# A thresholded attention kernel: who makes the threshold of a score tile, ScalarE or VectorE

## The chip, the core and the metric

The kernel runs on one core of one Trainium2 chip. The metric is the device time of one execution in microseconds (us). Engine names are those of the profile: PE is TensorE (PEld its weight loads), DVE is VectorE, ACT is ScalarE, POOL is GpSimd, SP is SyncE, which issues most of the DMAs. The granted clock of TensorE is 1.00 (2.4 GHz) in every stretch of the profile of the kernel before.

## The reference

There are 8 batches of 8 heads, each of 576 positions by 64. For every head the scores are thresholded a little below their row maximum, and what is left goes through a softmax; the heads of a batch, side by side, are the 512 columns of `x`, which a gated mix then turns into the output:

```
scores = q @ k.T / sqrt(64)
thresh = max(scores, axis=-1) - tau
scores = where(scores >= thresh, scores, -1e9)
attn   = exp(scores - max(scores)); attn = attn / (sum(attn) + 1e-9)
x      = attn @ v                        # the heads side by side
gate   = sigmoid(causal convolution of x with 5 taps per column)
out    = (gate * (x @ w_val)) @ w_out
```

## The kernel before, in words

Heads are taken in pairs: a **job** is one pair of one batch (32 jobs, 4 per batch). Each job has 9 score **tiles** of 128 rows by 576 columns, 288 in all: four of 128 queries for each head, and one in which both heads' last 64 queries share the rows.

What a tile goes through (`class Tile`):

- **scores** (`multiply`, L538 to L558, matmuls on L556): PE writes the tile into one of the PSUM rooms `r_s`, of which there are three for the first tiles and two from then on.
- **row maximum** (`largest`, L560 to L564, instruction on L562): DVE writes minus the maximum into the first column of a small tile `nm` (128x2).
- **exponential** (`weigh`, L566 to L572): ACT computes `e = exp(s - max)` (L568). With `TH = "ACT"` ACT issues a second instruction right behind it (L570): the threshold, `nm[:, 1] = -nm[:, 0] + less`, one element for each of 128 rows, where `less` is minus tau.
- **keep** (`keep`, L579 to L593, instruction on L589): DVE computes `(s >= nm[:, 1]) * e` with the row sums. It reads the PSUM room, `nm` and `e`, and its end gives all three back; PE's scores of a later tile wait for the room.
- After that POOL adds 1e-9 to the sums (L609), DVE inverts them (L611), POOL or ACT divides (L622, L618), PE transposes the tile in parts (L678), ACT copies each part to SBUF (L689, L694, L700), and PE multiplies by `v` (L752).

In the first batch the division is done behind the product with `v`, on DVE (L761), and the convolution by PE (L807); in the later batches the convolution is one tap on POOL (L847) and four on DVE (L854). The two products of the mix run on PE for each batch (L924), beside the attention of the next; those of the last batch come at the very end. Up to about 160 us DVE, ACT and POOL also unpack the weights (L258 to L302).

**The order of the work** is made ahead of time by a planner (`op`, L139, and `carry_out`, L153): every operation is entered with an engine, a due time in tiles, a cost (how long its engine is taken) and a time when its result is there. The planner goes through them by its own clock: on each engine, of those that can begin earliest, it takes the one with the lowest due time. The instructions are emitted in that order, and each engine runs its own queue in order. So a changed cost or a changed engine of one kind of operation changes the order of all queues. The operations of a tile `k` are due at `k - 8` (scores), `k - 8.5` (maximum and exponential) and `k - 8` (keep). Operations of DVE that share a port with POOL are entered as `"DVEp"`, and the planner keeps those and POOL's apart; the operations that the change touches are entered as plain `"DVE"`.

Of the kernel before, what the change touches and what calls it, by code (L numbers as in the profile page):

```python
# [18 lines left out]

P = 128  # L20
AHEAD = False
TH = "ACT"
DIVIDE = ("ACT",)
DUE = (8, 8.5, 8)
PACE_M = 0.17
# [24 lines left out]
def tile_thresholded_attention_gated_mix(  # L50
# [14 lines left out]
    nc = tc.nc  # L65
# [39 lines left out]
    class Op:  # L105
        def __init__(self, ways, due, after, takes, gives):
            self.ways, self.due = ways, due
            self.takes, self.gives = takes, list(gives)
            self.ready = 0.0
            self.waits = 0  # L110
            self.next = []
            self.landed = None
            for a in after:
                if a.landed is None:
                    a.next.append(self)
                    self.waits += 1
                else:
                    self.ready = max(self.ready, a.landed)
# [20 lines left out]
    def op(engine, due, cost, done, emit, after=(), takes=(), gives=(), other=()):  # L139

        shift = SHIFT.get((emit.__qualname__.split("<locals>.", 1)[1], engine))
        if shift:
            due += shift[sum(due >= p for p in PHASES)]
        ways = {w[0]: w[1:] for w in ((engine, cost, done, emit), *other)}
        o = Op(ways, due, after, takes, gives)
        if not o.waits:
            for e in ways:
                open_ops[e].append(o)  # L150
        return o
# [338 lines left out]
    class Tile:  # L490
        def __init__(self, k, t, h, qc, grp):
            self.k, self.t, self.h, self.qc, self.grp = k, t, h, qc, grp
            i = h or 0
            both = h is None
            if both:
                after = t.blocks if t.i == 0 else [t.high_k, t.low_k, *t.blocks]
            elif t.i == 0:
                after = [t.first[qc // 2][h]]
            else:
                after = t.copied  # L500
            if tiles:
                after = after + [tiles[-1].scores]
            gives = []
            if t.i == 0:
                gives = [(r_pre, t.lent)] if t.last == (h, qc) else []
            elif both:
                gives = [(r_kh, lambda: t.kh), (r_kl, lambda: t.kl), (r_bd, lambda: t.bd)]
            elif t.last == (h, qc):
                gives = [(r_Q, lambda: t.Q), (r_KH, lambda: t.KH), (r_KL, lambda: t.KL)]
            cost = 1.0 if t.i == 0 else 0.80 if both else 0.54  # L510
            self.scores = op(
                "PE", k - DUE[0], cost, cost + 0.26, self.multiply, after, [r_s], gives,
            )
            largest = op("DVE", k - DUE[1], 0.67, 0.84, self.largest, [self.scores], [r_nm])
            if TH == "ACT":
                after = [op("ACT", k - DUE[1], 0.83, 1.0, self.weigh, [largest], [r_e])]
            else:
                after = [
                    op("ACT", k - DUE[1], 0.64, 0.78, self.weigh, [largest], [r_e]),
                    op("DVE", k - 9, 0.13, 0.13, self.level, [largest]),  # L520
                ]
            room = [] if i else [r_pl if both else r_pp]
            if i:
                after.append(grp.kept)
            elif grp.after:
                after += grp.half.kept[-1:]
                room += [] if grp.half.kept else [r_all]
            else:
                room.append(r_sums)
            grp.kept = op(  # L530
                "DVE", k - DUE[2], 0.74, 0.96, self.keep, after, room,
                [(Scores(k), lambda: self.s), (r_e, lambda: self.e), (r_nm, lambda: self.nm)],
            )
            grp.keeps.append(grp.kept)
            if grp.after:
                grp.half.kept.append(grp.kept)
# [29 lines left out]
        def weigh(self):  # L566
            self.e = r_e.take()
            nc.scalar.activation(self.e, self.s[:, :, :HS], AF.Exp, bias=self.nm[:, 0:1])  # L568
            if TH == "ACT":
                nc.scalar.activation(  # L570
                    self.nm[:, 1:2], self.nm[:, 0:1], AF.Identity, bias=less, scale=-1.0
                )  # L572

        def level(self):
            nc.vector.tensor_scalar(
                self.nm[:, 1:2], self.nm[:, 0:1], -1.0, less, op0=ALU.mult, op1=ALU.add
            )

# [542 lines left out]
```

## Time and profile before

| what | value |
|---|---|
| median of the runs | 733.68 us (733.28 to 734.31) |
| the profiled execution | 734.48 us |
| its span, from the first to the last instruction | 732.6 us |
| outside the span | 1.88 us |
| busy: PE, DVE, ACT, POOL | 721.2, 600.3, 621.4, 530.1 us |
| score tiles, instructions on L570 | 288, 288 |

Busy time is the share of the span in which at least one instruction of the engine ran. The ends of matmuls overlap with the starts of the next, so 98% of busy PE is an upper bound of what it does. A wait is given with the instruction that ended it.

### The profile page before, as it was taken

What the parts mean: (1) busy time and instruction counts of PE and PEld (TensorE: products, weight loads), DVE (VectorE), ACT (ScalarE), POOL (GpSimd) and SP (SyncE); (2) the same over time, 40 slices, a digit from 0 to 9 for tenths busy, and PEclk for the clock granted to TensorE, in tenths of its full rate; (3) what the DMA queues carried; (4) which work ended last, traced back from release to release, by engine and by line L of the source; (5) the groups of instructions that cost most, each with busy time, mean ns of one, the idle gap of its engine ahead of it and who ended that gap; (6) DMA issues with size and microseconds to landing.
All of it is one profiled execution on the core that took longest, in us unless ns stands there. A gap on an engine that the chain in (4) does not pass through costs nothing.

```text
span 732.6 us, 16311 instructions
## 1 busy us (share of the span) xinstructions
PE 721.2 (98%) x5454; PEld 613.9 (84%) x5454; DVE 600.3 (82%) x1291; ACT 621.4 (85%) x1448; POOL 530.1 (72%) x886
## 2 busy tenths in 40 slices
PE   8989999999999999999999999999999999999998
PEld 4767778888898888888888888888888988888898
DVE  6899979999888888788888888888888888888730
ACT  6698889999899988888989889898989988888832
POOL 4876568778889757697778786897658887766331
PEclk9999999999999999999999999999999999999999
DMA  7755665636564655346655546555635465540001
GB/s 211 186 154 149 161 156 138 153 97 154 156 176 125 155 134 138 108 125 181 152 138 140 129 120 162 142 129 137 172 101 144 122 159 152 127 112 21 33 34 65
DMA packets 51588, 97.97 MB, mean 134 GB/s; under 512 B 9008, under 2 KB 9520, under 8 KB 51504
## 3 DMA queue, kind: packets, MB, share of 16 engines
q1 hardware_dynamic: 51264, 96.61, 51.1%
q8 instruction: 44, 0.72, 0.5%
q10 hardware_dynamic: 240, 0.31, 0.2%
q14 instruction: 40, 0.33, 0.1%
HBM read 34.62 MB, written 9.44 MB: 60 GB/s over the span
## 4 chain that ended last, share of the span: by engine, by line
PE 89%; ACT 4%; DVE 3%; DMA 2%; POOL 1%; issue 1%; SPq 0%; ACTq 0%; POOLq 0%
PE acc L924 26%; PE s L556 22%; PE acc L752 21%; PE tp L678 18%; ACT e L568 1%; PE acc L807 1%; DVE pp L589 1%; DVE nm L562 1%; DMA q_r<-qT 1%; ACT T L689 1%; DMA pre<-kT 0%; ACT pp L618 0%; ACT nm L570 0%; ACT xh L837 0%; DMA Q<-ql 0%
## 5 line engine op out<-in xcount | busy, mean ns | idle before, releaser
L562 DVE TENSOR_REDUCE nm<-s 128x1 f32<-128x576 f32 x288 | 214.1, 754 | 44.6 <-PE s L556 41.5
L589 DVE SCALAR_TENSOR_TENSOR pp<-s,nm,e 128x576 f32<-128x576 f32 x256 | 207.2, 813 | 33.2 <-ACT nm L570 29.2
L568 ACT ACTIVATE e<-s,nm 128x576 f32<-128x576 f32 x288 | 215.5, 748 | 19.8 <-DVE nm L562 14.8
L689 ACT COPY T<-tp 128x384 f32<-128x384 f32 x384 | 176.2, 487 | 26.2 <-PE tp L678 24.7
L678 PE MATMUL tp<-ident,pp 128*128 128x128 f32 x1152 | 175.3, 273 | 1.1 <-ACT T L689 1.1
L752 PE MATMUL acc<-T,v 128*64 128x256 f32 (+1 forms) x1280 | 169.3, 411 | 0.0
L622 POOL TENSOR_SCALAR pp<-pp,sums 128x576 f32<-128x576 f32 x165 | 137.6, 840 | 39.4 <-DVE sums L611 33.0
L556 PE MATMUL s<-KH,Q 128*128 128x288 f32 x496 | 152.2, 323 | 3.3 <-DVE pp L589 3.1
L678 PEld LDWEIGHTS tp<-ident,pp 128*128 128x128 f32 x1152 | 138.7, 140 | 7.2 <-ACT T L689 1.8
L556 PE MATMUL s<-KL,Q 128*128 128x288 f32 x496 | 138.2, 295 | 0.0
L752 PEld LDWEIGHTS acc<-T,v 128*64 128x64 f32 x1280 | 86.2, 136 | 61.5 <-issue 8.9
L556 PEld LDWEIGHTS s<-KH,Q 128*128 128x128 f32 x496 | 93.4, 188 | 29.0 <-issue 13.7
L854 DVE SCALAR_TENSOR_TENSOR pre<-xT,cw,pre 128x576 f32<-128x576 f32 x112 | 103.3, 922 | 9.1 <-POOL pre L847 8.9
L556 PEld LDWEIGHTS s<-KL,Q 128*128 128x128 f32 x496 | 93.6, 189 | 0.3
L570 ACT ACTIVATE nm<-nm,less 128x1 f32<-128x1 f32 x288 | 85.3, 296 | 0.0
L924 PE MATMUL acc<-gh,woh 128*128 128x320 f32 (+1 forms) x256 | 79.0, 309 | 0.0
L924 PE MATMUL acc<-xl,wvh 128*128 128x320 f32 (+1 forms) x256 | 78.5, 307 | 0.0
L924 PE MATMUL acc<-xh,wvl 128*128 128x320 f32 (+1 forms) x256 | 78.3, 306 | 0.0
L924 PE MATMUL acc<-xh,wvh 128*128 128x320 f32 (+1 forms) x256 | 78.0, 305 | 0.0
L924 PE MATMUL acc<-gl,woh 128*128 128x320 f32 (+1 forms) x256 | 77.9, 304 | 0.0
L924 PE MATMUL acc<-gh,wol 128*128 128x320 f32 (+1 forms) x256 | 77.5, 303 | 0.0
L609 POOL TENSOR_SCALAR sums<-sums 128x2 f32<-128x2 f32 (+1 forms) x144 | 39.7, 276 | 43.0 <-DVE pp L589 30.5
(99 smaller groups left out, 1241.8 us busy)
## 6 DMA issues: line engine op xcount, KB each, us to landing
KH<-kh SPq DMA_DIRECT2D x124, 144.0 KB, 2.6
KL<-kl SPq DMA_DIRECT2D x124, 144.0 KB, 2.9
v<-vs SPq DMA_DIRECT2D x32, 320.0 KB, 3.2
k_r<-kT SPq DMA_DIRECT2D x31, 320.0 KB, 3.8
q_r<-qT SPq DMA_DIRECT2D x31, 288.0 KB, 4.0
outT<-o SPq DMA_DIRECT2D x31, 288.0 KB, 2.1
Q<-qh SPq DMA_DIRECT2D x62, 128.0 KB, 2.3
Q<-ql SPq DMA_DIRECT2D x62, 128.0 KB, 2.4
```

The lines of the kernel that those rows point to most:

```text
L556: nc.tensor.matmul(s[:, a, :HS], w, m, start=i == 0, stop=i == len(terms) - 1)
L562: nc.vector.tensor_reduce(self.nm[:, 0:1], self.s[:, :, :HS], axis=AX.XY, op=ALU.max, negate=True)
L568: nc.scalar.activation(self.e, self.s[:, :, :HS], AF.Exp, bias=self.nm[:, 0:1])
L570: nc.scalar.activation(self.nm[:, 1:2], self.nm[:, 0:1], AF.Identity, bias=less, scale=-1.0)
L589: nc.vector.scalar_tensor_tensor(grp.p[:, i * S : (i + 1) * S].rearrange("p (a f) -> p a f", a=2), self.s[:, :, :HS], self.nm[:, 1:2], self.e,
L609: add = op("POOL", k - 4, 0.2, 0.33, lambda: nc.gpsimd.tensor_scalar(sums(), sums(), 1.0, 1e-9, op0=ALU.mult, op1=ALU.add), [self.kept])
L622: nc.gpsimd.tensor_scalar(v, v, ri(i), 0.0, op0=ALU.mult, op1=ALU.add)
L678: nc.tensor.transpose(tp[:, i * P : (i + 1) * P], self.p[:, k0 : k0 + P], ident)
L689: nc.scalar.copy(T[:, c0 : c0 + n, self.off : self.off + P], tp[:, 0 : n * P].rearrange("p (c q) -> p c q", q=P),)
L752: nc.tensor.matmul(acc[hs, :w], t.v[:, c0 : c0 + D], T[:, chunk, :], start=c == NKC, stop=c == NKC - 1, skip_group_check=True,)
L854: nc.vector.scalar_tensor_tensor(cv, t.xT[:, i : i + S], cw[:, g, i : i + 1], cv, op0=ALU.mult, op1=ALU.add)
L924: nc.tensor.matmul(taken[name, e, j][:, :w], wt[:, c, c0 : c0 + P], moving(c, i)[:, hs], start=n == 0, stop=n == NM - 1,)
```

## The change

`TH` becomes `"DVE"`. `weigh` then no longer issues the second ACT instruction, and the planner's cost of it falls from 0.83 to 0.64 us (its result from 1.0 to 0.78 us). A new operation `level` makes the same threshold with one `tensor_scalar` on DVE, behind the maximum, due at `k - 9`, with a planned cost of 0.08 us and a result after 0.16 us. `keep` now waits for both `weigh` and `level`. The branch for this was in the kernel already, unused, with other planned costs. No DMA is added, removed or moved to another queue.

```
-TH = "ACT"
+TH = "DVE"
...
                 after = [
                     op("ACT", k - DUE[1], 0.64, 0.78, self.weigh, [largest], [r_e]),
-                    op("DVE", k - 9, 0.13, 0.13, self.level, [largest]),
+                    op("DVE", k - 9, 0.08, 0.16, lambda: self.level(nc.vector), [largest]),
                 ]
...
-        def level(self):
-            nc.vector.tensor_scalar(
+        def level(self, on):
+            on.tensor_scalar(
                 self.nm[:, 1:2], self.nm[:, 0:1], -1.0, less, op0=ALU.mult, op1=ALU.add
             )
```

## Rows read from the trace of the kernel before

**Rows 1.** The page's first part: busy time of each engine, its share of the span, and its instructions.

```profile
PE 721.2 (98%) x5454; PEld 613.9 (84%) x5454; DVE 600.3 (82%) x1291; ACT 621.4 (85%) x1448; POOL 530.1 (72%) x886
```

**Rows 2.** Busy time by stretches of the span: start and end, length, then for PE, PEld, DVE, ACT and POOL the busy us and (in brackets) the instructions, the granted clock, the share of the DMA engines and GB/s.

```profile
40.00:70.00 30.00, 28.81 (x201) 22.57 (x202) 28.42 (x67) 26.63 (x67) 20.60 (x37) 1.00 0.56 152
70.00:92.00 22.00, 20.78 (x145) 16.78 (x145) 20.11 (x49) 19.72 (x49) 13.75 (x25) 1.00 0.64 159
110.00:140.00 30.00, 30.00 (x233) 25.57 (x231) 28.34 (x72) 28.18 (x65) 24.42 (x36) 1.00 0.59 148
140.00:184.00 44.00, 43.81 (x338) 37.34 (x337) 40.41 (x87) 41.01 (x98) 35.88 (x57) 1.00 0.51 125
184.00:690.00 506.00, 504.62 (x3933) 437.36 (x3932) 427.29 (x897) 447.57 (x1037) 386.95 (x630) 1.00 0.52 133
```

**Rows 3.** The same view for the row maximum on L562 alone, so that the number in brackets is that of the tiles in each stretch (the busy time before it is DVE's).

```profile
40.00:70.00 30.00, 9.08 (x13) 1.00 0.56 152
70.00:92.00 22.00, 7.38 (x10) 1.00 0.64 159
110.00:140.00 30.00, 9.16 (x13) 1.00 0.59 148
140.00:184.00 44.00, 13.42 (x18) 1.00 0.51 125
184.00:690.00 506.00, 157.29 (x212) 1.00 0.52 133
```

**Rows 4.** What PE's matmuls waited for, over the whole span: total us, times, the longest.

```profile
PE s L556 <- DVE pp L589: 5.4, 6, 1.2
PE tp L678 <- ACT T L689: 1.1, 4, 0.5
```

**Rows 5.** The last two of those six waits for `keep`, in the timeline of PE: start, length, instruction, and in brackets the idle time before it.

```profile
107.69 0.40 PE L556 MATMUL s<-KH,Q 128*128 128x288 f32 x1 [0.41 <-DVE pp L589]
303.67 0.40 PE L556 MATMUL s<-KH,Q 128*128 128x288 f32 x1 [1.20 <-DVE pp L589]
```

**Rows 6.** The chain of waits that ended last, as far as 184 us: its shares of that stretch by line, and then its pieces on L570 in order of time (start, length); there are 12 pieces, of which the first, the longest and the last stand here.

```profile
by line: PE s L556 20.7%; PE acc L752 17.1%; PE tp L678 14.6%; PE acc L924 10.9%; ACT e L568 4.3%; PE acc L807 4.1%; issue 3.0%; ACT T L689 2.8%; DVE nm L562 2.8%; DVE pp L589 2.8%; DMA pre<-kT 1.9%; DMA Q<-ql 1.4%; DMA KL<-kl 1.3%; ACT nm 
8.71 0.19 ACT nm L570
...
61.97 0.31 ACT nm L570
...
150.83 0.18 ACT nm L570
```

**Rows 7.** Groups of instructions by line: number, busy us, mean ns of one, then the idle time just before them and what ended most of it.

```profile
L562 DVE TENSOR_REDUCE nm<-s 128x1 f32<-128x576 f32 x288 | 214.1, 754 | 44.6 <-PE s L556 41.5
L589 DVE SCALAR_TENSOR_TENSOR pp<-s,nm,e 128x576 f32<-128x576 f32 x256 | 207.2, 813 | 33.2 <-ACT nm L570 29.2
L570 ACT ACTIVATE nm<-nm,less 128x1 f32<-128x1 f32 x288 | 85.3, 296 | 0.0
```

**Rows 8.** The timeline of ACT around one tile (start, length).

```profile
401.86 0.76 ACT L568 ACTIVATE e<-s,nm 128x576 f32<-128x576 f32 x1
402.50 0.30 ACT L570 ACTIVATE nm<-nm,less 128x1 f32<-128x1 f32 x1
402.68 0.59 ACT L694 COPY T<-tp 128x512 f32<-128x512 f32 x1
```

**Rows 9.** The timeline of DVE: the row maximum with a short instruction behind it, and a pair (L258, L260) of which the second reads what the first wrote.

```profile
400.79 0.76 DVE L562 TENSOR_REDUCE nm<-s 128x1 f32<-128x576 f32 x1
401.46 0.15 DVE L611 RECIPROCAL sums<-sums 128x2 f32<-128x2 f32 x1
...
23.59 0.08 DVE L589 DVE_READ_ACCUMULATOR pp<-s,nm,e 128x1 f32 x1
23.59 0.32 DVE L258 TENSOR_SCALAR spare_m<-o 128x256 int32<-128x256 int32 x1
23.94 0.47 DVE L260 SCALAR_TENSOR_TENSOR spare<-o,spare_m 128x256 int32<-128x256 int32 x1
```

**Rows 10.** The only one-element `TENSOR_SCALAR`s of DVE in the trace (number, then shortest, median and longest ns, first and last start), and POOL's instruction after them, with its idle time before it.

```profile
L1024 DVE TENSOR_SCALAR sc<-tau_sb x1: 154/154/154, 3.3 to 3.3; 128x1 f32<-128x1 f32 x1
L1027 DVE TENSOR_SCALAR less<-tau_sb x1: 145/145/145, 3.4 to 3.4; 128x1 f32<-128x1 f32 x1
4.73 0.56 POOL L244 TENSOR_SCALAR pre<-pre 64x64 f32<-64x64 f32 x2 [2.53 <-ACT pre L459]
```

**Rows 11.** A `TENSOR_SCALAR` of DVE beside POOL: the timelines of the two engines, then the group of that line with its shortest, median and longest duration.

```profile
36.86 0.74 POOL L377 TENSOR_SCALAR q_r<-q_r,sc 128x576 f32<-128x576 f32 x1
37.57 0.73 POOL L302 TENSOR_TENSOR wvl<-spare,wvh 128x256 fp32r<-128x256 f32 x1
36.95 1.51 DVE L258 TENSOR_SCALAR spare_m<-o 128x256 int32<-128x256 int32 x1
L258 DVE TENSOR_SCALAR spare_m<-o x16: 283/290/1508, 23.6 to 154.9; 128x256 int32<-128x256 int32 x16
```

**Rows 12.** The timeline of PE where it goes from transposes to scores.

```profile
401.16 0.38 PE L556 MATMUL s<-KH,Q 128*128 128x288 f32 x1
401.38 0.30 PE L556 MATMUL s<-KL,Q 128*128 128x288 f32 x1
401.51 0.30 PE L556 MATMUL s<-KH,Q 128*128 128x288 f32 x1
```

## The prediction

> **What bounds the kernel now.** I read the page's busy times first, then the same by stretches, then PE's waits, and last the chain of waits. PE is busy for 721.2 of 732.6 us, ACT for 621.4, DVE for 600.3 [rows 1]; the reader is to see that the change moves work between two engines that are not the fullest. By stretches there are two regimes. From 184 to 690 us PE is busy for 504.62 of 506 us, while DVE has 78.7 us to spare and ACT 58.4 [rows 2]: here PE is the bound, and nothing that DVE and ACT do matters unless it makes PE wait. Up to 184 us, where the weights are unpacked beside the first batches, DVE is as full as PE: 28.42 of 30 us from 40 to 70, 20.11 of 22 from 70 to 92, 28.34 of 30 from 110 to 140, 40.41 of 44 from 140 to 184 [rows 2].
>
> PE's own waits are few. Six times, 5.4 us in all, it waits for a `keep` to give back a PSUM room, four times, 1.1 us, for a copy by ACT [rows 4]. The fifth of the six is at 107.69 us, the last, of 1.20 us, at 303.67 [rows 5]. The chain of waits leaves PE more often than that: up to 184 us `e` on ACT has 4.3% of it, the maximum and `keep` on DVE 2.8% each, and twelve pieces are the ACT threshold itself [rows 6].
>
> **The change part by part.** *ACT loses 288 instructions.* One lasts 296 ns [rows 7], but it starts 0.12 us before the exponential ends, and the next copy starts 0.18 us after it does [rows 8]. So one takes 0.18 us of ACT's queue: 288 x 0.18 = 52 us, ACT's busy time falls to about 570 us. On the path that sets the end lie only the twelve pieces of the chain before 184 us, which are 0.18 to 0.31 us each and add up to 2.44 us [rows 6]. None lies on it later, where PE has no slack to give, so the other 276 are worth nothing there.
>
> *`keep` waits for less.* DVE idles 29.2 us at `keep` for the ACT threshold [rows 7]; now it waits for the exponential, which ends 0.18 us earlier (402.62 against 402.80 [rows 8]). This gives DVE time back; on the path it is already in the 2.44 us.
>
> *DVE gains 288 one-element instructions.* The trace has no such instruction in that place, so I bound it. Low end: DVE overlaps neighbours that don't depend on each other. The reciprocal at 401.46 starts 0.09 us before the maximum ahead of it ends, at 401.55, and lasts 0.15 us [rows 9]; the next would start as much before its end, so it takes 0.07 to 0.08 us. High end: one that reads what the one before it wrote starts after its end, as L260 at 23.94 behind L258, which ends at 23.91 [rows 9]. A threshold directly behind its maximum loses that overlap (0.12 us) and takes 0.07 us itself: 0.19, say 0.20 us. Which holds is the planner's choice: it knows that the maximum's result comes 0.17 us after DVE is free, and puts in between whatever else can begin. DVE is mostly full, so more thresholds should be like the reciprocal; I take 0.12 us, nearer to the low end, and keep 0.08 and 0.20 for the range. That is 288 x 0.12 = 35 us of DVE, from 600 to about 635.
>
> Here a page speaks against the change. The rows show overlap of 0.09 us between neighbours on DVE [rows 9]. The Trainium skill, VectorE: DVE Perf Modes, "The DRAIN you can't avoid", says that the next DVE operation does not issue until the pipe of the last has emptied, and advises fewer operations. By that a threshold would cost its full 0.15 us everywhere, 43 us in sum; this trace disagrees for neighbours that don't depend, and the sum goes by the rows.
>
> How much of it is on the path? Up to 184 us the chain has 5.6% of maxima and `keep`s, 10.3 us [rows 6]; one of each is 0.754 + 0.813 = 1.57 us [rows 7], so it passes DVE for about 6.6 tiles, and their thresholds add 6.6 x 0.12 = 0.8 us (0.5 to 1.3). Later DVE's spare 78.7 us [rows 2] cover 212 thresholds [rows 3], 25 us. If that cover were gone, they would be on the path.
>
> *The order.* With other costs the planner writes new queues for all engines. What that can move on PE is the number of times it goes from one kind of work to another: behind transposes the first scores matmul takes 0.22 us to the next, the second 0.13 [rows 12], so 0.09 us a change. If one tile in ten got one change more or less, that is 29 x 0.09 = 2.6 us, of either sign. I take zero and keep it for the range. The wait for two operations instead of one costs nothing of its own: the threshold is due before all else of its tile, and ahead of `e` unless a whole DVE instruction stands between. No DMA moves, and SP's and POOL's queues keep their operations.
>
> *The sum.* -2.44 + 0.8 = -1.6 us. When one path is shortened the next takes over, and before 184 us PE, DVE and ACT are nearly even; I keep half, -0.8 us. The profiled execution took 734.48 us and is 0.8 above the median of 733.68, so it becomes 733.7, and the median **732.9 us**. A measurement can tell this kernel from no change beyond about 0.2%, 1.5 us: below 732.2 or above 735.2. The forecast is no change, because PE is full for all but the start.
>
> **The rivals.** *Faster: the waits for the PSUM rooms go.* Each `keep` can end 0.2 to 0.3 us sooner, and ACT, 28.18 of 30 us busy at 110 to 140 [rows 2], is relieved of several thresholds in a row before some waits. If two thirds of PE's 5.4 us of waits for `keep` [rows 4] went, it would be 733.7 - 3.6 = 730.1 us; if all, 728.3. For it: five of the six waits are where ACT is on the chain. Against: the longest is as likely the DVE's own backlog.
>
> *Slower: DVE becomes the bound before 184 us.* The four full stretches have 1.58 + 1.89 + 1.66 + 3.59 = 8.7 us of idle DVE [rows 2] and 54 tiles [rows 3]. If half of that idle time can be used, 4.4 us, it decides at 4.4 / 54 = 0.08 us per threshold. At 0.20 us they need 10.8 us: 6.4 too much, and less the 2.4 us that ACT gives back it is 4.0 us, 737.7 us. For it: 0.08 is my low end, and DVE has fewer spare places just there. Against: a full DVE is just where the planner finds something to put between maximum and threshold.
>
> *Much slower: thresholds wait for POOL.* A `TENSOR_SCALAR` of DVE with both operands in SBUF, as the threshold is, lasted 1.51 us in place of 0.28 when it began while POOL's instructions ran until 38.30 [rows 11]. The planner does not keep the threshold apart from POOL's work. POOL is busy for 72% [rows 1] with instructions of some 0.8 us (0.73 and 0.74 in [rows 11]), so a threshold would wait 0.72 x 0.4 = 0.3 us more: 0.38 us each. In the four stretches that needs 20.5 us, 11.8 more than the idle time, and from 184 on 212 x 0.38 = 80.6 against 78.7, 1.9 more; less 2.4 this gives 745 us. The two one-element instructions in the trace took 154 and 145 ns, but POOL was idle beside them [rows 10], so the trace does not exclude it; with one element there is little to split between two ports. The Trainium skill, SBUF — State Buffer, "Who interferes with whom", states that `tensor_scalar` with SBUF operands can take the port pair that DVE shares with GpSimd, and whoever comes second waits for the whole instruction. By that the sum would be this rival's; the trace agrees for 256 elements [rows 11], and no run here shows it for one.
>
> **How the numbers follow.** No change 0.36; faster 0.33; slower 0.31, of which 0.22 DVE's backlog and 0.09 POOL. The order of the queues blurs all of them by its 2.6 us. The range takes in the faster case down to 728.5 (all six waits) and the slower one up to 740 (737.7 and most of the 2.6), and leaves out POOL's rival: 728.5 to 740. Cases of both signs hold most of the chance; the forecast's own range is 731.5 to 735.
>
> **What would show it.** No ACT instruction on the threshold's line, ACT busy near 570 us, DVE near 635 (about 620 at 0.08 us, 660 at 0.20, 700 with POOL's waits). Threshold durations near 0.15 us speak against the POOL rival, a long tail up to 1 us for it. DVE's waits at `keep` now name `e`, and are shorter in all. If PE's idle time before 184 us is about as before, and from 184 to 690 us near 1.4 us, the forecast's mechanism holds. It is wrong if PE's idle or its count of changes moves by more than 1.5 us: then the order of the queues, not the price of the threshold, decided.

## The result, and the profile after

| kernel | median us | ratio to before (95% interval) |
|---|---|---|
| before | 733.48 | |
| after | 742.51 (742.30 to 743.37) | 1.0122 [1.0109, 1.0135] |

The kernel became 1.2% slower: 9.0 us, outside the range that ended at 740. Its profiled execution took 742.3 us with a span of 740.4, against 734.48 and 732.6 before.

First the page's first part for the kernel after; [rows 1] are the same of before.

```profile
PE 726.6 (98%) x5454; PEld 616.5 (83%) x5454; DVE 629.8 (85%) x1579; ACT 604.1 (82%) x1205; POOL 495.3 (67%) x841
```

DVE has 288 instructions and 29.5 us more, as it should. ACT has only 17.3 us less, where 52 were expected, and POOL has lost 45 instructions and 34.8 us, though the edit touches nothing of POOL's. PE does the same 5,454 matmuls in a span 7.8 us longer and is still 98% busy.

The groups show where ACT's relief went. The first six rows are of after, in the form of [rows 7] (busy us, mean ns | idle time before them and what ended it).

```profile
L562 DVE TENSOR_REDUCE nm<-s 128x1 f32<-128x576 f32 x288 | 212.1, 751 | 40.2 <-PE s L556 38.1
L589 DVE SCALAR_TENSOR_TENSOR pp<-s,nm,e 128x576 f32<-128x576 f32 x256 | 207.0, 813 | 18.4 <-ACT e L568 12.4
L575 DVE TENSOR_SCALAR nm<-nm,less 128x1 f32<-128x1 f32 x288 | 56.8, 207 | 1.4
L622 POOL TENSOR_SCALAR pp<-pp,sums 128x576 f32<-128x576 f32 x131 | 109.5, 839 | 53.2 <-DVE sums L611 37.2
L618 ACT ACTIVATE pp<-pp,sums 128x576 f32<-128x576 f32 x93 | 72.0, 779 | 7.1 <-DVE sums L611 6.5
L618 ACT ACTIVATE pl<-pl,sums 128x576 f32<-128x576 f32 x16 | 12.5, 780 | 0.8 <-DVE sums L611 0.6
```

ACT's divisions (of full tiles, `pp`, and of the tiles that two heads share, `pl`) stand in the kernel before as follows.

```profile
L618 ACT ACTIVATE pp<-pp,sums 128x576 f32<-128x576 f32 x59 | 46.2, 784 | 4.7 <-DVE sums L611 4.6
L618 ACT ACTIVATE pl<-pl,sums 128x576 f32<-128x576 f32 x5 | 3.9, 781 | 1.6 <-DVE sums L611 1.6
```

The planner may give a division to POOL or to ACT. It saw ACT cheaper and gave it 109 of the 256 divisions in place of 64, 34.4 us more work (84.5 against 50.1); these 45 are the instructions that POOL lost. So every queue was written anew, and this was a real part of the change that the diff doesn't show. Where this text says "the order", it means the planner's whole plan: the order of every queue, and the engine of each division. The wait of DVE at `keep` is shorter (18.4 us against 33.2 [rows 7]), and what ends it is now the exponential: that step came as predicted.

Now by stretches, in the columns of [rows 2]: the kernel before, then the kernel after.

```profile
0.00:184.00 184.00, 177.30 (x1226) 140.32 (x1227) 161.23 (x374) 157.92 (x379) 132.63 (x244) 1.00 0.60 156
690.00:734.00 44.00, 39.30 (x299) 36.26 (x297) 11.82 (x21) 15.92 (x35) 10.50 (x13) 1.00 0.11 43
```

```profile
0.00:184.00 184.00, 175.35 (x1187) 137.70 (x1189) 163.79 (x438) 145.87 (x301) 124.91 (x238) 0.99 0.59 156
184.00:690.00 506.00, 504.19 (x3908) 435.94 (x3906) 449.03 (x1110) 436.62 (x861) 355.72 (x586) 1.00 0.52 132
690.00:742.00 52.00, 47.03 (x365) 42.89 (x359) 17.02 (x33) 21.58 (x45) 14.64 (x18) 1.00 0.12 46
```

The reader should count the matmuls and leave the busy time aside. By 184 us PE has done 39 fewer than before (1187 against 1226), between 184 and 690 us another 25 fewer (3908 against 3933 [rows 2]), and 66 more remain for the end. In the long stretch PE's busy time is the same to 0.4 us: there a matmul that starts late lengthens the busy time of the row and not its idle time. At 506 / 3920 = 0.13 us a matmul the 25 are 3.2 us; the 39 at 175.35 / 1187 = 0.15 us are 5.8, of which 1.95 us are idle time of PE (8.65 us in place of 6.70).

The same loss by tiles: the row maxima are counted in order from 0, and the start of each before is taken from its start after.

| tile | 12 | 24 | 36 | 84 | 240 | 258 | 282 |
|---|---|---|---|---|---|---|---|
| us later | -1.6 | 4.1 | 4.8 | 5.7 | 6.7 | 9.0 | 5.6 |

Between these the difference goes up and down (8.2 us at 90, 2.8 at 132), so a single tile says little; most of it is there by tile 36.

PE's two largest sums of waits, in the form of [rows 4]:

```profile
PE s L556 <- DVE pp L589: 4.1, 10, 1.8
PE tp L678 <- ACT T L689: 2.2, 3, 1.2
```

All of its waits come to 10.1 us in 21 places, against 7.8 in 12 before. So the waits that the profile shows account for 2.3 of the 9 us, and none is longer than 1.8. Two causes were possible: the threshold on DVE itself, or the new order.

### The profile page after: what moved, and what is told of

It reads as the page before. It is cut to its first block, busy times and chain, and to the rows that moved or that the text cites. A ratio compares the mean times of both kernels' runs of the same rounds, so it can differ in the third digit from the quotient of the medians.

```text
span 740.4 us, 16524 instructions
## 1 busy us (share of the span) xinstructions
PE 726.6 (98%) x5454; PEld 616.5 (83%) x5454; DVE 629.8 (85%) x1579; ACT 604.1 (82%) x1205; POOL 495.3 (67%) x841
## 4 chain that ended last, share of the span: by engine, by line
PE 79%; DVE 8%; POOL 5%; ACT 5%; issue 3%; DMA 1%; SPq 0%; ACTq 0%; POOLq 0%; DVEq 0%
PE acc L924 22%; PE acc L752 20%; PE s L556 20%; PE tp L678 15%; DVE pp L589 3%; DVE nm L562 2%; ACT e L568 2%; PE acc L807 2%; DVE pre L854 1%; ACT T L689 1%; POOL pp L622 1%; POOL pre L794 1%; POOL ql L321 1%; POOL gl L321 1%; DMA pre<-qT 0%
## 5 line engine op out<-in xcount | busy, mean ns | idle before, releaser
L562 DVE TENSOR_REDUCE nm<-s 128x1 f32<-128x576 f32 x288 | 212.1, 751 | 40.2 <-PE s L556 38.1
L568 ACT ACTIVATE e<-s,nm 128x576 f32<-128x576 f32 x288 | 213.3, 750 | 26.5 <-DVE nm L562 20.6
L589 DVE SCALAR_TENSOR_TENSOR pp<-s,nm,e 128x576 f32<-128x576 f32 x256 | 207.0, 813 | 18.4 <-ACT e L568 12.4
L678 PE MATMUL tp<-ident,pp 128*128 128x128 f32 x1152 | 177.6, 273 | 2.5 <-ACT T L689 1.5
L752 PE MATMUL acc<-T,v 128*64 128x256 f32 (+1 forms) x1280 | 169.3, 411 | 0.0
L622 POOL TENSOR_SCALAR pp<-pp,sums 128x576 f32<-128x576 f32 x131 | 109.5, 839 | 53.2 <-DVE sums L611 37.2
L752 PEld LDWEIGHTS acc<-T,v 128*64 128x64 f32 x1280 | 86.2, 137 | 60.9 <-issue 6.1
L609 POOL TENSOR_SCALAR sums<-sums 128x2 f32<-128x2 f32 (+1 forms) x144 | 41.5, 288 | 62.0 <-DVE pp L589 47.7
L924 PE MATMUL acc<-xh,wvl 128*128 128x320 f32 (+1 forms) x256 | 79.4, 310 | 0.0
L924 PE MATMUL acc<-gh,woh 128*128 128x320 f32 (+1 forms) x256 | 79.0, 309 | 0.2 <-ACT gh L969 0.2
L924 PE MATMUL acc<-xh,wvh 128*128 128x320 f32 (+1 forms) x256 | 79.1, 309 | 0.0
L924 PE MATMUL acc<-xl,wvh 128*128 128x320 f32 (+1 forms) x256 | 78.7, 307 | 0.0
L924 PE MATMUL acc<-gh,wol 128*128 128x320 f32 (+1 forms) x256 | 78.5, 307 | 0.0
L924 PE MATMUL acc<-gl,woh 128*128 128x320 f32 (+1 forms) x256 | 77.9, 304 | 0.0
L618 ACT ACTIVATE pp<-pp,sums 128x576 f32<-128x576 f32 x93 | 72.0, 779 | 7.1 <-DVE sums L611 6.5
```

The lines of the kernel that those rows point to most:

```text
L562: nc.vector.tensor_reduce(self.nm[:, 0:1], self.s[:, :, :HS], axis=AX.XY, op=ALU.max, negate=True)
L589: nc.vector.scalar_tensor_tensor(grp.p[:, i * S : (i + 1) * S].rearrange("p (a f) -> p a f", a=2), self.s[:, :, :HS], self.nm[:, 1:2], self.e,
L609: add = op("POOL", k - 4, 0.2, 0.33, lambda: nc.gpsimd.tensor_scalar(sums(), sums(), 1.0, 1e-9, op0=ALU.mult, op1=ALU.add), [self.kept])
L618: nc.scalar.mul(v, v, ri(i))
L622: nc.gpsimd.tensor_scalar(v, v, ri(i), 0.0, op0=ALU.mult, op1=ALU.add)
L678: nc.tensor.transpose(tp[:, i * P : (i + 1) * P], self.p[:, k0 : k0 + P], ident)
```

## The experiments

**Order and engine apart.** *Order theory:* the queues as the planner rewrote them cost the time, and the engine of the threshold little. *Threshold theory:* 288 more instructions on a DVE that is full at the start cost it, in whatever order. The first two kernels cross the two. One keeps every queue as before and lets DVE do the threshold where ACT did; in the other all queues are those of after, but ACT does it behind the exponential. The planner goes by its costs and not by what an instruction does, so neither edit moves anything else (in the traces all four queues have the same instructions in the same order, but for the threshold).

```
e1_old_order_dve, from the kernel before:
-                nc.scalar.activation(
-                    self.nm[:, 1:2], self.nm[:, 0:1], AF.Identity, bias=less, scale=-1.0
+                nc.vector.tensor_scalar(
+                    self.nm[:, 1:2], self.nm[:, 0:1], -1.0, less, op0=ALU.mult, op1=ALU.add

e2_new_order_act, from the kernel after:
-                    op("DVE", k - 9, 0.08, 0.16, lambda: self.level(nc.vector), [largest]),
+                    op("DVE", k - 9, 0.08, 0.16, lambda: None, [largest]),
-            if TH == "ACT":
+            if True:
```

Expected of `e1_old_order_dve`, then of `e2_new_order_act`:

> The queues of PE, POOL and SP and all other instructions in the order of the kernel before; only the threshold is made by DVE, entered in DVE's queue where the exponential was entered in ACT's. If the planner's order is the cause of the 9 us, this takes 732 to 736 us. If the threshold on DVE is the cause (208 ns each in the profile after, 288 of them), it takes 740 us or more.

> All queues in the order of the changed kernel; only the threshold is made by ACT behind the exponential, as in the kernel before, and DVE has none. If the order is the cause, this stays at 740 us or above (ACT gets its 52 us back, so it may even be slower than the changed kernel). If the threshold on DVE is the cause, it comes back to 732 to 736 us.

| | order of before | order of after |
|---|---|---|
| threshold on ACT | 734.04 (before) | 755.11, 1.0306 [1.0265, 1.0347] |
| threshold on DVE | 736.91, 1.0043 [1.0026, 1.0060] | 742.51 (after) |

The threshold on DVE costs 2.9 us in the order made for ACT and saves 12.6 in the order made for DVE; the order alone costs 5.6 us with DVE and 21 with ACT. The 736.91 us fall between the two expectations (732 to 736, and 740 or more), so the loss isn't the order's alone: on the way from before over `e1_old_order_dve` to after, the threshold on DVE has 2.9 us and the order 5.6. On the way over `e2_new_order_act` the order has more than the whole. Neither engine is cheaper as such: the one for which the queues were written is. The first part of the page of `e1_old_order_dve`, its waits of PE for `keep`, and its stretches up to 690 us:

```profile
PE 723.4 (98%) x5454; PEld 614.3 (84%) x5454; DVE 625.9 (85%) x1579; ACT 580.9 (79%) x1160; POOL 530.8 (72%) x886
```

```profile
PE s L556 <- DVE pp L589: 5.6, 7, 1.6
```

```profile
0.00:184.00 184.00, 177.72 (x1218) 139.47 (x1219) 166.53 (x446) 146.57 (x302) 131.53 (x242) 1.00 0.61 155
184.00:690.00 506.00, 504.49 (x3927) 436.67 (x3925) 445.49 (x1107) 417.20 (x824) 388.62 (x631) 1.00 0.52 133
```

With the old queues ACT falls to 580.9 us and POOL stays at 530.8. PE is 6 matmuls behind in the stretch (3927 against 3933 [rows 2]), not 25.

**The order alone.** If the order decides, the kernel before with its own instructions but other queues must move as far. Its planned cost of the exponential with the threshold was changed by 0.01 or 0.02 us, far less than the real durations scatter (the exponential alone took 0.72 to 0.84 us in the kernel before).

```
-                after = [op("ACT", k - DUE[1], 0.83, 1.0, self.weigh, [largest], [r_e])]
+                after = [op("ACT", k - DUE[1], 0.82, 0.99, self.weigh, [largest], [r_e])]   e3_order_a
+                ...                            0.85, 1.02                                    e4_order_b
+                ...                            0.84, 1.01                                    e9_order_c
+                ...                            0.81, 0.98                                    e10_order_d
```

Expected of these four, in the same order:

> The kernel before, instruction for instruction, with the planner's cost of exponential and threshold 0.82 us in place of 0.83 (result after 0.99 us), so that only the order of the queues differs. If order alone is worth several us, this lies over 2 us away from the kernel before, on the slow side more likely than not; if order alone is worth little, it stays within 1.5 us of 733.5.

> As the run with 0.82 us, with 0.85 us (result after 1.02 us): the same instructions in another order again. Order theory: over 2 us away from the kernel before and another time than with 0.82. Threshold theory: within 1.5 us of 733.5.

> The kernel before, instruction for instruction, planned with 0.84 us (result after 1.01 us) for exponential and threshold: a third new order with the threshold on ACT. If the recorded order of the kernel before is an unusually good one, this too takes 740 to 750 us; if the two new orders so far were unlucky, 732 to 738 us.

> As the run with 0.84 us, planned with 0.81 us (result after 0.98 us): a fourth new order with the threshold on ACT. Same expectation: 740 to 750 us if the order of the kernel before is unusually good, 732 to 738 us if not.

And the kernel after with other planned costs of its threshold; 0.13 and 0.25 us are about what DVE's timeline shows for it:

```
-                    op("DVE", k - 9, 0.08, 0.16, lambda: self.level(nc.vector), [largest]),
+                    op("DVE", k - 9, 0.13, 0.25, lambda: self.level(nc.vector), [largest]),   e5_real_costs
+                    ...              0.09, 0.17                                               e6_new_order_b
+                    ...              0.07, 0.15                                               e11_new_order_c
+                    ...              0.10, 0.18                                               e12_new_order_d
```

Expected of these four, in the same order:

> The changed kernel, its threshold entered in the planner with the cost that the profile after shows (0.13 us of DVE, result after 0.25 us, in place of 0.08 and 0.16). If the loss comes from planned costs that are too low, it is faster than 740 us. If any new order costs as much as any other, it lies anywhere from 738 to 750 us.

> The changed kernel, its threshold entered with 0.09 and 0.17 us in place of 0.08 and 0.16, a change of the planner's order alone. If order is what counts, it lies over 2 us from 742.5 us on either side; if the threshold on DVE has a price of its own that counts, within 1.5 us of it.

> The changed kernel planned with 0.07 us (result after 0.15 us) for the threshold: another order with the threshold on DVE. If the threshold on DVE helps once the order of the kernel before is set aside, this and its like have a mean 2 us or more below that of the new orders with ACT: 738 to 744 us. If the threshold on DVE has a price that counts, they are as slow or slower: 744 to 750 us.

> The changed kernel planned with 0.10 us (result after 0.18 us) for the threshold: a further order with the threshold on DVE, with the same two expectations: 738 to 744 us, or 744 to 750 us.

| planned cost, result | threshold on ACT | | planned cost, result | threshold on DVE | |
|---|---|---|---|---|---|
| 0.83, 1.00 (before) | 733.5 to 734.0 | | 0.08, 0.16 (after) | 742.51 | 1.0122 [1.0109, 1.0135] |
| 0.82, 0.99 | 747.48 | 1.0187 [1.0167, 1.0207] | 0.13, 0.25 | 740.46 | 1.0098 [1.0083, 1.0113] |
| 0.85, 1.02 | 741.97 | 1.0111 [1.0095, 1.0128] | 0.09, 0.17 | 742.36 | 1.0118 [1.0102, 1.0135] |
| 0.84, 1.01 | 742.98 | 1.0127 [1.0111, 1.0143] | 0.07, 0.15 | 740.31 | 1.0099 [1.0080, 1.0118] |
| 0.81, 0.98 | 746.45 | 1.0181 [1.0163, 1.0200] | 0.10, 0.18 | 745.62 | 1.0153 [1.0129, 1.0177] |

The same work as before in another order takes 8 to 13 us more. That is as much as the whole loss of the change, with ACT still making the threshold. All four tries went the same way, and so did every other kernel here whose queues were written anew: the order of before is an unusually good one among its neighbours, and each of these edits gave it up. The four other orders with ACT have a mean of 744.7 us, the five with DVE 742.3: nothing shows the threshold on DVE to be slower once both are in orders of that kind. That it is faster isn't shown either, since each group scatters by 5 us. The planned cost nearest to DVE's real price (0.13, 0.25) is no better than 0.07, 0.15.

These runs are not "instruction for instruction" the kernel before, as was expected of them: on their pages POOL has 11, 13, 24 and 20 instructions fewer than before, and ACT as many more, which are divisions. With DVE, 33 to 49 moved (45 in after). The time doesn't go with that number (747.48 us with 11 moved, 742.98 with 24; 745.62 with 37, 740.31 with 49). But no run keeps the divisions in place under a new order, so what their move costs by itself stays open.

One expectation missed, and one pair split. `e6_new_order_b` fell within 0.2 us of after, where the order theory wanted more; by itself it spoke for the threshold theory. `e12_new_order_d`, at 745.62 us, is in the range in which the threshold on DVE would have a price (744 to 750), and `e11_new_order_c`, at 740.31, in the other (738 to 744). These two differ by 5.3 us for planned costs 0.03 apart, clear of their intervals, so the nearness of `e6_new_order_b` to after is most likely chance.

What makes an order bad is not always the same. These are the page of `e3_order_a`, 747.48 us, and what its PE waited for most:

```profile
PE 725.3 (97%) x5454; PEld 615.5 (82%) x5454; DVE 606.0 (81%) x1291; ACT 628.2 (84%) x1459; POOL 520.4 (70%) x875
```

```profile
PE s L556 <- DVE pp L589: 13.5, 12, 2.6
```

Here the waits for `keep` are 13.5 us, 8.1 more than before [rows 4]; in `e4_order_b` they are 7.5 us, in after 4.1. The kernel after loses in smaller pieces. I took the distance from each matmul's start to the next, from 184 to 690 us, sorted the pairs by line and shape, and counted what exceeds the lower quartile of its kind of pair by over 40 ns. The product with `v` (L752, about 99 us in both kernels) is left out. That gives 26.2 us before (277 times) and 31.4 after (322 times). Of the 5.2 us of growth 3.7 are between two matmuls of the mix's products (L924): 10.7 us in 125 places before, 14.4 in 165 after. Each of these places is the first matmul of an unbroken series of products, and there are 212 such series before and 253 after: the new order cuts the products into more pieces, at about 0.09 us a piece. Over the whole span PE goes from one kind of work to another 938 times before and 991 after. But the counts don't rank kernels: `e3_order_a` has 922 such changes, and `e5_real_costs`, at 740.46 us, has 305 series of products.

The granted clock is a part of it too. Its mean over the profiled execution is 1.00 before, 0.998 in after and 0.995 in `e6_new_order_b` and `e10_order_d`; as an estimate, (1 - 0.995) x 744 = 3.7 us at most in the last two, and 1.5 in after. It isn't needed for a loss: `e4_order_b` and `e2_new_order_act` kept 1.00 and took 741.97 and 755.11 us.

**Where along the run.** The three kernels that follow start with one engine for the threshold and go on with the other, and the planner knows it.

```
from the kernel after, in the planned operations and in weigh:
-            if TH == "ACT":
+            if k < 72:       m1_dve_from_72   (k >= 72: m2_act_from_72; k < 144: m3_dve_from_144;
...                                             in weigh with self.k in place of k)
```

Expected of `m1_dve_from_72`, `m2_act_from_72` and `m3_dve_from_144`:

> Tiles 0 to 71 as in the kernel before (threshold on ACT), tiles 72 to 287 as in the changed one; the queues are those of the kernel before as far as about 165 us. If the loss is made while the weights are unpacked and no engine has room (39 of the 64 matmuls that the changed kernel is behind at 690 us), about 60% of it goes: 736 to 738 us. If it is made in the start alone, 733.5 to 735 us; if any new order costs the same wherever it begins, 740 us or more.

> Tiles 0 to 71 as in the changed kernel, tiles 72 to 287 with the threshold on ACT: the start is that of the changed kernel, the rest is a new order. If the start makes 60% of the loss and a new order makes the rest, 741 to 746 us; if the start alone makes it all, 742 to 743 us, and if the start makes none, 738 us or less.

> Tiles 0 to 143 as in the kernel before, the second half as in the changed one. If a new order costs in proportion to what is left of the run where PE is the bound, about 1.5 us: 735 to 736 us. If the start alone counts, 733.5 to 734.5 us.

| threshold on DVE | us | ratio |
|---|---|---|
| nowhere (before) | 733.41 | |
| from tile 144 on | 736.16 | 1.0041 [1.0026, 1.0056] |
| from tile 72 on | 739.70 | 1.0086 [1.0065, 1.0106] |
| everywhere (after) | 742.51 | 1.0122 [1.0109, 1.0135] |
| up to tile 71 | 745.63 | 1.0172 [1.0139, 1.0204] |

The loss grows with the part that is planned anew: 2.8 us from tile 144 on, 6.3 from tile 72 on, 9.1 in all. So a loss needs no change at the start. It doesn't follow that the tiles 72 to 143 of after cost 3.5 us: each of these kernels is a new order of its own, and new orders scatter by 5 us. In the trace of after itself 39 of the 64 matmuls are lost by 184 us, that is about 5.8 of the 9 us. `m1_dve_from_72` was expected at 736 to 738 and came out higher, since I held the start for most of it. `m2_act_from_72` lies in its range of 741 to 746, and `m3_dve_from_144` 0.2 us above its own. The next two fences are the stretches up to and from about tile 144, of before and of `m3_dve_from_144`, whose queues are the same up to about 349 us, with its first stretch.

```profile
184.00:366.00 182.00, 180.74 (x1409) 156.32 (x1408) 152.37 (x320) 162.16 (x376) 144.14 (x238) 1.00 0.57 145
366.00:690.00 324.00, 323.88 (x2526) 281.04 (x2526) 274.93 (x578) 285.40 (x662) 242.82 (x393) 1.00 0.50 127
```

```profile
0.00:184.00 184.00, 177.98 (x1227) 140.30 (x1228) 161.19 (x374) 157.97 (x379) 132.49 (x244) 1.00 0.60 155
184.00:366.00 182.00, 181.92 (x1418) 157.48 (x1418) 154.38 (x331) 162.07 (x371) 144.34 (x239) 1.00 0.56 146
366.00:690.00 324.00, 322.85 (x2500) 279.01 (x2497) 286.46 (x708) 280.30 (x551) 220.28 (x361) 1.00 0.49 126
```

At the start it is level with before (1227 matmuls, 1226 there). Behind the turn POOL falls by 22.5 us, ACT by only 5.1, and PE gets through 26 matmuls fewer, 3.3 us at 0.13, in a stretch where it is 99.6% busy. Against these stand 9 that it was ahead in the stretch between (1418 against 1409). `m2_act_from_72` shows that an order can also lose by going back: it has DVE's start and ACT's rest and is slower than either.

**One place of the start.** The timelines of POOL, DVE and PE of after show the longest of the early losses (start, length, instruction; in brackets the idle time before it).

```profile
33.11 1.92 POOL L794 TENSOR_SCALAR pre<-ident,cw 128x128 f32<-128x128 f32 x5
35.01 0.56 POOL L244 TENSOR_SCALAR bdq<-ql 64x64 fp32r<-64x64 f32 x2
35.67 1.76 POOL L794 TENSOR_SCALAR pre<-ident,cw 128x128 f32<-128x128 f32 x5
37.52 0.20 POOL L714 TENSOR_SCALAR all<-all 128x4 f32<-128x4 f32 x1
37.75 0.18 DVE L717 RECIPROCAL all<-all 128x4 f32<-128x4 f32 x1 [3.30 <-POOL all L714]
37.84 0.80 DVE L589 SCALAR_TENSOR_TENSOR pp<-s,nm,e 128x576 f32<-128x576 f32 x1
38.71 0.40 PE L556 MATMUL s<-KH,Q 128*128 128x288 f32 x1 [1.79 <-DVE pp L589]
```

Ten diagonal matrices (L794) stand in POOL's queue ahead of one instruction on four sums (L714). DVE waits 3.30 us for those sums with `keep` behind them, and PE waits 1.79 us for `keep`'s room. The kernel before has the same ten matrices ahead of the same sums, and its sums come even later:

```profile
32.41 3.78 POOL L794 TENSOR_SCALAR pre<-ident,cw 128x128 f32<-128x128 f32 x10
38.39 0.20 POOL L714 TENSOR_SCALAR all<-all 128x4 f32<-128x4 f32 x1
38.62 0.18 DVE L717 RECIPROCAL all<-all 128x4 f32<-128x4 f32 x1 [0.17 <-POOL all L714]
```

There DVE waits 0.17 us, because other work stands in its queue ahead of their inverses (L717). So what the new order changed at this place is DVE's queue: it comes to L717 at 34.45 us, with nothing to do before POOL is through. A second loss follows from the first. By stretches of 3 us, after:

```profile
36.00:39.00 3.00, 1.21 (x9) 0.97 (x9) 1.25 (x5) 0.41 (x1) 2.84 (x9) 1.00 1.05 226
39.00:42.00 3.00, 3.00 (x12) 2.61 (x12) 2.96 (x8) 2.57 (x5) 3.00 (x4) 0.51 0.53 124
42.00:45.00 3.00, 3.00 (x21) 2.73 (x19) 1.79 (x7) 1.74 (x5) 2.00 (x5) 0.92 0.20 44
```

After 3 us in which PE was busy for 1.21, the granted clock (the third number from the end) is 0.51, the 1.2 GHz level, for the next 3 us, and PE, busy all the time, gets through 12 matmuls. In the kernel `e7_taps_later` only the ten matrices were moved behind the sums in POOL's queue:

```
+                while held:
+                    held.pop(0)()                      # behind the half's sums
...
-        ready = op("POOL", k - 12, 1.0, 1.1, spread_taps, [conv_ready])
+        def later():
+            held.append(spread_taps)
+        ready = op("POOL", k - 12, 1.0, 1.1, later if g >= 2 else spread_taps, [conv_ready])
```

> The changed kernel with one thing moved in POOL's queue: the ten diagonal matrices of the convolution that stand ahead of the half's sums near 33 us come right behind them and their spreading; all else stays in its order. If the loss up to the 24th tile comes from that place in the order, DVE's wait of 3.3 us and PE's of 1.8 us near 38 us go, the granted clock stays at 1.00, and the kernel takes 738 to 740 us; 742.5 us if that place was covered anyway.

It took 741.16 us, 1.0103 [1.0088, 1.0118]. The same stretches of it:

```profile
36.00:39.00 3.00, 3.00 (x23) 2.69 (x20) 2.54 (x6) 2.38 (x6) 3.00 (x9) 1.00 1.03 251
39.00:42.00 3.00, 2.67 (x18) 2.22 (x17) 2.97 (x7) 2.16 (x6) 3.00 (x5) 1.00 0.28 94
```

The gap is gone, and with it the low clock; tile 30 is 0.5 us behind before instead of 2.4. But of the 2 us gained there 1.35 are left at the end, with intervals that overlap, less than the 2.5 to 4.5 I had expected. The place is real and is only a small part.

**The price of the threshold.** This kernel is `e1_old_order_dve` with the same `tensor_scalar` issued twice in a row.

> The order of the kernel before, the threshold on DVE, made twice in a row for each tile. One threshold on DVE cost 2.9 us in this order. If that is DVE's time on the path, the second costs 2 to 4 us more: 739 to 741 us. If it is a wait at one or two places, the second is nearly free: 737 to 738 us.

It took 764.62 us, 1.0415 [1.0398, 1.0433]: 27.7 us more than with one. I expected 2 to 4, or almost nothing; both theories missed. Its page, what its PE waited for most, and a piece of its DVE timeline follow (the threshold is on L570, the second one on L573, `keep` on L592).

```profile
PE 738.0 (97%) x5454; PEld 616.4 (81%) x5454; DVE 678.3 (89%) x1867; ACT 583.4 (77%) x1160; POOL 527.0 (69%) x886
```

```profile
PE s L556 <- DVE pp L592: 12.6, 23, 1.9
```

```profile
420.71 0.21 DVE L570 TENSOR_SCALAR nm<-nm,less 128x1 f32<-128x1 f32 x1
420.95 0.21 DVE L573 TENSOR_SCALAR nm<-nm,less 128x1 f32<-128x1 f32 x1
421.27 0.82 DVE L592 SCALAR_TENSOR_TENSOR pp<-s,nm,e 128x576 f32<-128x576 f32 x1
```

The second begins 0.24 us after the first, so 288 of them take 69 us of DVE, and PE's waits for `keep` go from 5.6 us (7 times) to 12.6 (23 times). The first threshold cost the run 2.9 us, the second 27.7. So in that order DVE has room for one and not for two; the 78.7 us of idle DVE that [rows 2] give from 184 to 690 us are not 78.7 us to spare. Over the whole span 41.5 us of DVE's idle time stand before a row maximum that waits for its scores [rows 7], and a late `keep` makes the next scores late. Not all of the loss can be followed so: PE's idle time grows from 11.1 us (734.5 of span less 723.4 busy) to 22.2 (760.2 less 738.0), and the rest of the 25.7 us between the two spans doesn't show as idle time.

## Why the prediction was wrong, point by point

**The step that failed is "The order".** It took zero, with 2.6 us of either sign as its bound, from one tile in ten with one change of PE more or less. The order alone moves this kernel by 8 to 13 us, and always up in four tries: both the size and the even sign were wrong. The bound counted one mechanism (changes of PE) on a guessed share of tiles: 29 changes, where 53 came, 4.8 us by my price. It left out that a new order brings other waits for `keep` (13.5 us in `e3_order_a`), that it moves divisions between POOL and ACT (45 in after), and that DVE's queue can hold up the start (3.30 us at L717), with a low clock behind it. The prediction's own sign of being wrong came: PE's idle time before 184 us rose by 1.95 us and its changes by 53, both beyond 1.5 us, so the order decided more than the price of the threshold.

**The sum, -1.6 us and halved -0.8:** of the wrong sign by itself. With the queues held it is +2.9 us [1.9, 4.4] (`e1_old_order_dve`). Two readings under it were wrong by little: the chain has a thirteenth piece of L570, 0.19 us at 302.57, where I wrote that none lies later; and by [rows 9] the low end is 0.15 - 0.09 = 0.06 us, not 0.07 to 0.08. PE is 8 matmuls behind at 184 us (1218 against 1226, 1.2 us at 0.15) and 14 at 690: the thresholds' share of the path is larger than the 0.8 us that I gave it, and goes on behind 184 us.

**"Nothing that DVE and ACT do matters unless it makes PE wait", after 184 us:** wrong as I used it. PE's idle time there stayed at 1.8 us (1.4 before), yet 25 matmuls were lost, about 3.2 us: the busy share couldn't show it. And `m1_dve_from_72`, whose queues are those of before up to about 178 us, loses 6.3 us.

**"ACT's busy time falls to about 570 us":** it is 604.1. With the old queues it fell to 580.9, 40.5 us for 288, or 0.14 us each in place of the 0.18; the other 23.2 us came with the 45 divisions that the planner moved to ACT (34.4 us by their rows, less what they overlap their neighbours and what else changed there). I had written that the queues of POOL keep their operations. That was wrong: 45 left it.

**"DVE gains 35 us":** nearly right. It gained 29.5 (25.6 with the old queues), 0.10 and 0.09 us each; the other instructions of DVE lasted 3.7 us less in sum, so a threshold added about (29.5 + 3.7) / 288 = 0.12 us, the value that I took. That the two ends were both too low, with the instruction at 0.21 us and not 0.15, didn't show in the mean. Behind an instruction on which it doesn't depend the threshold starts before that ends, and the next one 0.13 us after the threshold, where I had 0.08; behind its own maximum it starts late, and the next one 0.13 us after it again. Both in DVE's timeline of after:

```profile
39.29 0.74 DVE L562 TENSOR_REDUCE nm<-s 128x1 f32<-128x576 f32 x1
40.07 0.21 DVE L575 TENSOR_SCALAR nm<-nm,less 128x1 f32<-128x1 f32 x1
40.20 0.75 DVE L562 TENSOR_REDUCE nm<-s 128x1 f32<-128x576 f32 x1
...
401.93 0.82 DVE L589 SCALAR_TENSOR_TENSOR pp<-s,nm,e 128x576 f32<-128x576 f32 x1
402.67 0.08 DVE L589 DVE_READ_ACCUMULATOR pp<-s,nm,e 128x1 f32 x1
402.67 0.21 DVE L575 TENSOR_SCALAR nm<-nm,less 128x1 f32<-128x1 f32 x1
402.80 0.81 DVE L854 SCALAR_TENSOR_TENSOR pre<-xT,cw,pre 128x576 f32<-128x576 f32 x1
```

At 40.07 it begins 0.04 us after its maximum has ended. At 402.67 it begins 0.08 us before `keep` (401.93 + 0.82) ends. In both places the next instruction begins 0.13 us after the threshold began, before its 0.21 us are over. The Trainium skill, VectorE: DVE Perf Modes, "The DRAIN you can't avoid", says that the next operation does not start until the pipe empties, and adds that one that is not held starts earlier; the prediction gave the first half alone. The trace agrees with the second half, at both places.

**The rival "DVE becomes the bound"** (737.7 us, 0.22) named a real mechanism: with the old queues the time is 736.9, and with two thresholds 764.6. That 736.9 is so close to its price is luck in part, since 6 of the 14 matmuls lost there are lost behind 184 us and not where the rival put them. And it isn't what made most of the loss of the change.

**The rival "thresholds wait for POOL"** fell. By line, all 288 thresholds of after (shortest, median and longest ns):

```profile
L575 DVE TENSOR_SCALAR nm<-nm,less x288: 183/208/217, 7.3 to 699.1; 128x1 f32<-128x1 f32 x144
```

There is no tail, with POOL 67% busy. The Trainium skill, SBUF — State Buffer, "Who interferes with whom", says that a `tensor_scalar` can contend for the shared ports, and that the one that comes second is blocked; a wait of that kind is seen at 256 elements [rows 11] and in none of the 288 thresholds.

**The rival "the waits for the rooms go":** they fell from 5.4 to 4.1 us in total but from 6 to 10 in number. It was worth 1.3 us at most.

**What stays open:** why the order of before is so much better than its neighbours, and how much of a new order's price is that of the moved divisions. Waits for `keep`, places where the mix's products are cut up, stretches at a low clock, and one stall at the start each explain a part of some kernel; no single count ranks all of them.

## What to carry to other kernels

Where a planner writes the queues, a changed cost is a change of its own. Try it in the old order with the new instruction, and in a few new orders with the old one, before saying what the edit is worth; here the order alone moved the time by up to 13 us, and the engine alone by 3 in the order that was there. Where the planner also chooses between engines, look whether other instructions changed engines. When an engine is 98% busy, count its instructions in a stretch of before and after, since late starts of overlapped instructions don't show as idle time. Idle time of an engine that mostly waits for its input isn't room for more work.

## What the runs showed of the hardware

- A one-element `TENSOR_SCALAR` of DVE that takes its second operand from SBUF lasted 208 ns at the median, not the 145 to 154 ns of [rows 10]. What makes the difference wasn't tried.
- Of two one-element instructions of DVE that write the same column, the second began 0.24 us after the first began; behind an unrelated instruction the next started 0.13 us after the threshold.
- In the kernel after the granted clock fell to 0.51 in one stretch of 3 us, after one with PE busy for 1.21 of 3 us, and was 1.00 in the same stretch of the kernel in which that gap was closed.
